# Sets of many products kept apart in a list schedule, and a GLU's tokens split anew for each group of f

## The chip, the cores and the metric

One Trainium2 chip, one core. The metric is the device time of one execution in microseconds, as a median over runs; one more execution was taken with the hardware profiler. Its engines are named as in the profile: PE (TensorE's matmuls), PEld (its weight loads), DVE (VectorE), ACT (ScalarE), POOL (GpSimd, here memsets and issuing DMAs) and SP (SyncE, here only issuing DMAs).

## The reference

A gate mixes a state-space convolution (S4D) with a bilinear GLU; L = 2048 tokens, D = 512 channels, N = 128 states, F = 1792:

```python
g = sigmoid((u * gate_w).sum(-1, keepdims=True))
P = exp((A * dt[:, None])[:, :, None] * pos)          # A, C complex, (D, N)
K = 2 * einsum("dn,dnl->dl", C, P).real               # the kernel of the convolution
a = irfft(rfft(u.T, 2 * L) * rfft(K, 2 * L))[:, :L].T + u * D_skip
b = ((x @ w_gate) * (x @ w_up)) @ w_down
return g * a + (1 - g) * b
```

All is float32.

## The kernel before

**The GLU.** x comes transposed (xT) in four blocks ci of 512 tokens, each as KT = 4 tiles of 128 x 512. Its products run in a faster float format (F32R) at three products each: every operand is split into a high part (ACT casts the loaded tile `raw` to `xhi`) and a low part (DVE subtracts: `xlo` = `raw` - `xhi`), and hi x lo, lo x hi and hi x hi are summed. The 14 tiles of f are taken in five groups of three or two (`GROUPS`); each group goes over all four ci, to and fro, so that of the four ci of a group after the first three need their tokens again. For each f, 24 products give `pg` and `pu` (gate and up), ACT and DVE make h = pg * pu and split it into `hh` and `hl`, and products with the split down weights (`dhi`, `dlo`) add up in `y`. Each group's y is scaled by 1 - g (`acc`) and stored to or added to the output in memory by a DMA; the last block's y is added in SBUF to what was loaded into `kt` (`ends`).

Where do the tokens come from? `tokens_first` (group 0) loads xT into `raw`, splits it, and POOL stores both halves in device memory (`x_d`). `tokens_again` (later groups) has SP load the two halves from `x_d`. `raw` has two buffers, shared with the loads of weights; `xhi` and `xlo` have five each.

**The convolution.** u goes through a first Fourier step (`u_part`, eight sets `k<-in,w_t`). For 16 blocks of 32 channels DVE and ACT build tables `x` and `v`, whose products make the convolution's kernel (`k_block`, `kgen`: `k<-v,x`). Every fourth block, `k_first` transforms it (`k<-kt,w1k_t`), and `transforms(q)` does the rest for a quarter q of the channels: four second steps (`m_second`: `k<-in,w2s`, in the last quarter `k<-v,w2s` with `k<-x,w2s`), the product of spectra on DVE, two inverse steps (`m_inverse`: `k<-y,w3s`), each followed by stores to `y_d`, loads from `y_d`, and two last steps (`m_last`: `k<-in,w_t`, in the last quarter `k<-v,w_t`). Then the gate is applied and POOL adds the result to the output.

A **set** is what one such task issues on TensorE. `kgen`, `m_second` and `m_inverse` issue 64 small float32 matmuls on parts of the array; the profile shows each as two pairs of a weight load and a matmul, so a set has 128 pairs. `k_first` issues sets of 16 and 48 pairs; `u_part` and `m_last` only 8.

**What sets the order.** Nothing is issued directly. `add` records a Task with an engine, an assumed time, tiles read and written, a rank and, for DMAs, kilobytes. `Work.run` is a list scheduler: it keeps a time for each engine and one for the bus, and of all tasks whose inputs are there and whose buffers come free it takes the one that can start first, then the lowest rank; GLU products have rank 2, sets 1, 0 or -1. The tasks are issued in that order, and each engine keeps it (`InOrder`). So the table of assumed times decides the order on every engine, and nothing else about the run.

Of the kernel before, what the change touches and what calls it, by code (L numbers as in the profile page):

```python
# [10 lines left out]
F32 = mybir.dt.float32  # L11
F32R = mybir.dt.float32r
# [6 lines left out]
P = 128  # L19
# [119 lines left out]
class Task:  # L139
    def __init__(self, n, engine, us, fn, rank, after, dma):  # L140
        self.n, self.engine, self.us, self.fn, self.rank, self.after, self.dma = n, engine, us, fn, rank, after, dma
        self.deps, self.tiles, self.start, self.end, self.rows = set(), [], None, None, ()


class Work:
# [10 lines left out]
    PE_LAG = 0.17  # L156

    OVERLAP = {"act": 0.09, "dve": 0.08}
    DMA_RATE = 0.3

    def __init__(self):
# [5 lines left out]
    def memory(self):  # L167
        return Tile(self, None, None, None, None, None, False)

    def add(self, engine, us, fn, r=(), w=(), rank=1, after=0.0, dma=0, hold=(), rows=()):  # L170


        task = Task(len(self.tasks), engine, us, fn, rank, after, dma)
        task.rows = rows
        self.tasks.append(task)
        clash = lambda p, q: p is None or q is None or p == q
        split = lambda x: x if isinstance(x, tuple) else (x, None)
        for tile, part in map(split, r):
            task.deps.update(t for p, t in tile.writers if clash(p, part))
        for tile, part in map(split, w):  # L180
            task.deps.update(t for p, t in tile.writers + tile.readers if clash(p, part))
        for tile, part in map(split, r):
            tile.readers.append((part, task))
        for tile, part in map(split, w):
            tile.writers.append((part, task))
        for tile, _ in map(split, [*r, *w, *hold]):
            if tile.pool and tile not in task.tiles:
                task.tiles.append(tile)
                tile.users.append(task)
        task.deps.discard(task)  # L190
        return task
# [34 lines left out]
    def run(self):  # L226
        left = {}
        for t in self.tasks:
            left.setdefault(t.engine, []).append(t)
        free = {e: 0.0 for e in left}  # L230
        bus, order, known, rows = 0.0, [], {}, {}
        while any(left.values()):
            best, wanted, found = None, {}, []
            for e, tasks in left.items():
                for t in tasks:
                    at = known.get(t)
                    if at is None:
                        at = self.inputs(t)
                        if at is None:
                            continue  # L240
                        known[t] = at
                    found.append((t, at))
                    for tile in t.tiles:
                        if tile.loose and tile.made is None:
                            wanted.setdefault(tile.key, []).append((t.rank, at))
            for t, ins in found:
                at = self.slots(t, ins)
                if at is None:
                    continue
                start = max([at, free[t.engine]] + [rows[r] for r in t.rows if r in rows])  # L250
                if any(
                    rank < t.rank and when <= start
                    for tile in t.tiles if tile.made is None and tile.loose for rank, when in wanted[tile.key]
                ):
                    continue
                key = (start, t.rank, t.n)
                if best is None or key < best[0]:
                    best = (key, t)
            assert best, "no work can start"
            (start, _, _), t = best  # L260
            left[t.engine].remove(t)
            t.start, t.end = start, start + t.us
            free[t.engine] = t.end - self.OVERLAP.get(t.engine, 0.0)
            if t.dma:
                bus = max(bus, t.end + 1.3) + t.dma / self.DMA_RATE / 1000
                t.end = bus + 0.5
            rows.update((r, t.end) for r in t.rows)
            for tile in t.tiles:
                if tile.made is None:
                    tile.made = start  # L270
                    tile.had.append(tile)
            order.append(t)
        for t in order:
            t.fn()
        return order
# [3 lines left out]
def gated_mix_kernel(  # L279
# [29 lines left out]
    su_d = dram.tile([KT, P, 32, P], F32, name="su_d")  # L309
    sk_d = dram.tile([KT, P, 32, P], F32, name="sk_d")  # L310
    y_d = dram.tile([KT, P, 32, P], F32, name="y_d")
    x_d = dram.tile([4, KT, 2, P, D], F32, name="x_d")
    m_su, m_sk, m_y, m_out = (work.memory() for _ in range(4))
    m_x = {}

    pools = {n: open_pool(n, b, PSUM) for n, b in (("ps_y", 2), ("ps_g", 1), ("ps_k", 4))}
    const = open_pool("const")
# [69 lines left out]
    def load_two(key, tile_of, src, one=True):  # L387

        t = tile_of([P, 2, D])
        for k in range(2):  # L390
            raws[key(k)] = (t, k)
        if one:
            add("sp", 0.42, lambda: sp.dma_start(t.t, src), w=[t], dma=512, rank=-1)
        return t
# [3 lines left out]
    def first_loads():  # L398
        in_y = lambda shape: new("mid", "y", shape, bufs=2)
        in_ev = lambda shape: new("mid", "ev", shape, bufs=3)  # L400
        xsrc = lambda kt: xT[P * kt : P * kt + P, :D]
        w0 = load_two(lambda k: ("w", 0, k), in_ev, None, False)
        x01 = load_two(lambda k: ("x", 0, k), in_y, None, False)
        for t, k, src in ((x01, 0, xsrc(0)), (w0, 0, wts[0][:, :D]), (w0, 1, wts[0][:, D : 2 * D]), (x01, 1, xsrc(1))):
            add("sp", 0.42, lambda t=t, k=k, src=src: sp.dma_start(t.t[:, k], src), w=[(t, k)], dma=256, rank=-1)
        x23 = xT[2 * P : 4 * P, :D].rearrange("(k p) t -> p k t", k=2)
        load_two(lambda k: ("x", 0, 2 + k), in_y, x23)
        for f in (1, 2):
            load_two(lambda k, f=f: ("w", f, k), in_ev, wts[f][:, : 2 * D].rearrange("p (k d) -> p k d", k=2))


        zero = new("glu", "acc", [P, D], bufs=3)
        scratch = bank()
        add("dve", 0.2, lambda: dve.memset(zero.t, 0.0), w=[zero], rank=-1)

        def warm():
            for _ in range(3):
                pe.matmul(scratch.t, zero.t[:, :P], zero.t, start=True, stop=True)

        add("pe", 4.0, warm, r=[zero], w=[scratch], rank=-1)  # L420

    def weights(fs):
        for f in fs:
            ws[f] = [new("glu", n, [P, 2 * D], F32R, len(GROUPS[0])) for n in ("whi", "wlo")]
            for c in range(2):
                load(("w", f, c), wts[f][:, c * D : (c + 1) * D])
                split(ws[f][0], ws[f][1], c, ("w", f, c))
            if f == 0:
                for kt in range(1, KT):
                    tokens_first(0, kt)  # L430

    def down_weights(fs):
        for f in fs:
# [1 line left out]
            load(("w", f, 2), wts[f][:, 2 * D :])  # L435
            split(wd[f][0], wd[f][1], None, ("w", f, 2))

    def tokens_first(ci, kt):

        x = xs[kt] = [new("glu", n, [P, D], F32R, 5) for n in ("xhi", "xlo")]  # L440
        load(("x", ci, kt), xT[kt * P : (kt + 1) * P, ci * D : (ci + 1) * D])
        split(x[0], x[1], None, ("x", ci, kt))
        for k in range(2):
            m = m_x[ci, kt, k] = work.memory()
            add("pool", 0.95, lambda k=k: pool_q.dma_start(x_d[ci, kt, k], x[k].t.bitcast(F32)), r=[x[k]], w=[m], dma=256)

    def tokens_again(ci, kt):
        x = xs[kt] = [new("glu", n, [P, D], F32R, 5) for n in ("xhi", "xlo")]
        for k in range(2):
            add(  # L450
                "sp", 0.42, lambda k=k: sp.dma_start(x[k].t.bitcast(F32), x_d[ci, kt, k]),
                r=[m_x[ci, kt, k]], w=[x[k]], dma=256, rank=0,
            )

    THREE = ((1, 0), (0, 1), (0, 0))

# [101 lines left out]

    def glu():
        order = [(gi, ci) for gi in range(len(GROUPS)) for ci in (range(4) if gi % 2 == 0 else range(3, -1, -1))]  # L560
        tokens_first(0, 0)
        weights(GROUPS[0])
        down_weights(GROUPS[0])
        old = 0
        for n, (gi, ci) in enumerate(order):
            fs = GROUPS[gi]
            if ci != old:
                for kt in range(KT):
                    (tokens_again if gi else tokens_first)(ci, kt)
            old = ci  # L570
            hs = {f: hidden(f) for f in fs}
            ends = n % 4 == 3 and gi + 1 < len(GROUPS)
# [346 lines left out]
    def k_block(b, x, v):  # L919
# [12 lines left out]
        if b % 4 == 0:  # L932
            kts["now"] = new("tab", "kt", [P, 64, 32])
        kt, g0 = kts["now"], b % 4 * 8
        add("pe", 2.15, kgen, r=[x, v], w=[pk], rank=0, hold=[kt])
        add(
            "act", 1.09,
            lambda: act.copy(
# [7 lines left out]
    def k_first(q, kt):  # L946

        tt(0.19, lambda: kt.t[:, 48, :], lambda: kt.t[:, 48, :], lambda: skip[:, q], ALU.add, [m_skip], [kt])
        for h in range(2):
# [14 lines left out]
                            )  # L964
                    to += n

            add("pe", 2.08, fn, r=[kt, m_w1k], w=banks, rank=-1, hold=sts)
            for half in range(2):

                st = sts[half]  # L970
# [56 lines left out]
    def m_second(q, ins, w):  # L1027
# [15 lines left out]
                                    start=True, stop=True, tile_position=(64 * e, 32 * j),  # L1043
                                )

        add("pe", 2.13, fn, r=[*ins, w], w=banks[0] + banks[1], rank=1, hold=tos)
        for which in range(2):
            for e in range(2):
                to, bk = tos[which], banks[which][e]
# [37 lines left out]
    def m_inverse(q, T0, ys, ws):  # L1087
# [14 lines left out]
                                    ys[t].t[lanes, k, e, cs], start=k == 0, stop=k == 1, tile_position=(32 * j, 64 * e),  # L1102
                                )

        add("pe", 2.13, fn, r=[*ys, *ws], w=banks, rank=1, hold=sts)
        for j in range(4):
            st, m = sts[j // 2], j % 2
            evict(
# [189 lines left out]
```

## Time and profile before

| | us |
|---|---|
| median of 3 runs (lowest to highest) | 633.33 (632.41 to 633.38) |
| the profiled execution's own time | 631.22 |
| its span, first to last instruction | 629.4 |
| PE's last product ends | 625.4 |
| DMA traffic | 142.63 MB, 227 GB/s |

Every instruction has line L100, that of the helper which issues it, so the profile is read by tile names: `out<-in`. "Issue" is time in which an engine waited for nothing that the profile shows. Matmuls overlap, so that a product's own duration (0.39 us) is longer than the distance from one to the next. In the chain in order of time, merged pieces give that distance: length divided by count.

### The profile page before, as it was taken

To read this page: it belongs to the slowest core of one execution; us is meant where nothing else is said; L and a number is where in the kernel's file an instruction comes from. 1 tells how busy PE (TensorE), PEld (TensorE's weight loads), DVE (VectorE), ACT (ScalarE), POOL (GpSimd) and SP (SyncE) were. 2 spreads that over 40 slices of the span, in tenths; PEclk is the share of its full clock that TensorE was granted. 3 is DMA by queue.
4 is the path that set the end of the run, shared out by engine and by line. 5 is a ranking of instruction groups with operands and counts; after the bars stand their busy time and mean duration, and the time that the engine had idled before them with its cause. 6 is when DMAs were issued, how large, how long until landed. Compare 5 with 4: busy or idle time off the path is not lost.

```text
span 629.4 us, 17934 instructions
## 1 busy us (share of the span) xinstructions
PE 608.8 (97%) x7526; PEld 469.1 (75%) x7526; DVE 486.1 (77%) x760; ACT 397.0 (63%) x903; POOL 106.1 (17%) x157
## 2 busy tenths in 40 slices
PE   7899999999999999999999999999999998999997
PEld 5667768688687787877777887778787676786885
DVE  6858999999999898999999999899853255632113
ACT  5379778968787764887977687796544542222220
POOL 3143332211021110202110101201010030102210
PEclk9999999999999999999999999999999999999999
DMA  8899868557879697969998398899889598958841
GB/s 310 266 338 334 298 191 317 180 164 238 231 184 284 179 240 224 223 200 257 196 321 219 93 247 264 210 222 275 242 239 326 171 245 215 280 152 193 161 68 67
DMA packets 111892, 142.63 MB, mean 227 GB/s; under 512 B 7876, under 2 KB 66756, under 8 KB 111556
## 3 DMA queue, kind: packets, MB, share of 16 engines
q1 hardware_dynamic: 90100, 105.05, 52.9%
q0 software_dynamic: 21568, 36.45, 28.1%
q8 instruction: 59, 0.97, 0.6%
q14 instruction: 21, 0.17, 0.1%
q10 hardware_dynamic: 144, 0.00, 0.0%
HBM read 81.96 MB, written 59.51 MB: 225 GB/s over the span
## 4 chain that ended last, share of the span: by engine, by line
PE 89%; DMA 5%; issue 2%; DVE 2%; ACT 1%; SPq 0%; ACTq 0%; DVEq 0%
PE pu L100 23%; PE pg L100 23%; PE y L100 23%; PE k L100 20%; DMA raw<-in_xT 2%; DMA raw<-in_wts 2%; DMA xlo<-x_d 1%; DVE x L100 1%; DMA small<-in_rows 1%; DVE kt L100 0%; ACT ts L100 0%; ACT acc L100 0%; ACT xhi L100 0%; ACT dhi L100 0%; SPq L100 0%
## 5 line engine op out<-in xcount | busy, mean ns | idle before, releaser
L100 POOL DMA_DIRECT2D out<-acc x60 | 51.4, 901 | 357.9 <-ACT acc L100 333.1
L100 PE MATMUL pg<-xhi,wlo 128*128 128x512 f32 x224 | 89.7, 401 | 2.9 <-DVE wlo L100 1.8
L100 PE MATMUL y<-dhi,hl 128*128 128x512 f32 x224 | 89.7, 401 | 2.7 <-DVE hl L100 2.4
L100 PE MATMUL pu<-xhi,wlo 128*128 128x512 f32 x224 | 90.1, 402 | 0.4 <-issue 0.4
L100 PE MATMUL pg<-xlo,whi 128*128 128x512 f32 x224 | 87.9, 392 | 1.9 <-issue 1.2
L100 PE MATMUL pu<-xlo,whi 128*128 128x512 f32 x224 | 87.4, 390 | 0.0
L100 PE MATMUL y<-dhi,hh 128*128 128x512 f32 x224 | 87.4, 390 | 0.0
L100 PE MATMUL pg<-xhi,whi 128*128 128x512 f32 x224 | 87.3, 390 | 0.0
L100 PE MATMUL y<-dlo,hh 128*128 128x512 f32 x224 | 87.3, 390 | 0.0
L100 PE MATMUL pu<-xhi,whi 128*128 128x512 f32 x224 | 87.3, 390 | 0.0
L100 DVE TENSOR_TENSOR h<-pu,h 128x512 f32<-128x512 f32 x56 | 38.5, 688 | 59.4 <-PE pu L100 58.3
L100 ACT ACTIVATE acc<-y,ngate 128x512 f32<-128x512 f32 x76 | 52.1, 690 | 34.6 <-PE y L100 31.7
L100 ACT CAST hh<-h 128x512 fp32r<-128x512 f32 x56 | 34.7, 620 | 59.6 <-DVE h L100 59.6
L100 ACT COPY ts<-k 128x512 f32<-128x512 f32 (+1 forms) x116 | 48.8, 497 | 19.9 <-PE k L100 19.9
L100 ACT COPY h<-pg 128x512 f32<-128x512 f32 x56 | 32.9, 588 | 41.8 <-PE pg L100 37.5
L100 PEld LDWEIGHTS pg<-xhi,wlo 128*128 128x128 f32 x224 | 42.0, 188 | 19.4 <-issue 5.0
L100 PEld LDWEIGHTS y<-dhi,hl 128*128 128x128 f32 x224 | 42.0, 187 | 17.9 <-DVE hl L100 4.1
L100 PEld LDWEIGHTS pu<-xhi,wlo 128*128 128x128 f32 x224 | 42.0, 187 | 17.3 <-issue 8.3
L100 PEld LDWEIGHTS pg<-xlo,whi 128*128 128x128 f32 x224 | 42.1, 188 | 11.6 <-issue 1.6
L100 PEld LDWEIGHTS pu<-xhi,whi 128*128 128x128 f32 x224 | 42.1, 188 | 9.1
L100 PEld LDWEIGHTS y<-dhi,hh 128*128 128x128 f32 x224 | 42.0, 188 | 9.1
L100 PEld LDWEIGHTS pg<-xhi,whi 128*128 128x128 f32 x224 | 42.1, 188 | 9.0
(105 smaller groups left out, 1127.6 us busy)
## 6 DMA issues: line engine op xcount, KB each, us to landing
out<-acc POOLq DMA_DIRECT2D x60, 256.0 KB, 6.0
xhi<-x_d SPq DMA_DIRECT2D x48, 256.0 KB, 5.1
xlo<-x_d SPq DMA_DIRECT2D x48, 256.0 KB, 5.2
raw<-in_wts SPq DMA_DIRECT2D x36, 256.0 KB, 4.6
su_d<-ts POOLq DMA_DIRECT2D x32, 256.0 KB, 5.1
sk_d<-ts SPq DMA_DIRECT2D x16, 512.0 KB, 4.6
y_d<-ts SPq DMA_DIRECT2D x16, 512.0 KB, 5.7
in<-sk_d SPq DMA_DIRECT2D x12, 512.0 KB, 6.4
```

The source lines that it names most:

```text
L100: got = getattr(self.engine, name)(*args, **kw)
```

## The change

A task can be marked `many`. `kgen`, `k_first`, `m_second` and `m_inverse` are. The scheduler keeps a time `apart`: a marked task doesn't start before the end of the last marked one plus `APART` = 4.0 us of its own clock. And `tokens_first`, `tokens_again`, `x_d` and its stores go; one function `tokens` loads xT and splits it in every group (`raws` is a table of loads already asked for, so the group is now part of its key).

```diff
+    APART = 4.0
...
-        task.rows = rows
+        task.rows, task.many = rows, many
...
-                start = max([at, free[t.engine]] + [rows[r] for r in t.rows if r in rows])
+                start = max([at, free[t.engine], apart * t.many] + [rows[r] for r in t.rows if r in rows])
...
             left[t.engine].remove(t)
+            if t.many:
+                apart = start + t.us + self.APART
...
-    def tokens_first(ci, kt):
+    def tokens(gi, ci, kt):
         x = xs[kt] = [new("glu", n, [P, D], F32R, 5) for n in ("xhi", "xlo")]
-        load(("x", ci, kt), xT[kt * P : (kt + 1) * P, ci * D : (ci + 1) * D])
-        split(x[0], x[1], None, ("x", ci, kt))
-        for k in range(2):
-            m = m_x[ci, kt, k] = work.memory()
-            add("pool", 0.95, lambda k=k: pool_q.dma_start(x_d[ci, kt, k], x[k].t.bitcast(F32)), r=[x[k]], w=[m], dma=256)
-
-    def tokens_again(ci, kt):
-        x = xs[kt] = [new("glu", n, [P, D], F32R, 5) for n in ("xhi", "xlo")]
-        for k in range(2):
-            add(
-                "sp", 0.42, lambda k=k: sp.dma_start(x[k].t.bitcast(F32), x_d[ci, kt, k]),
-                r=[m_x[ci, kt, k]], w=[x[k]], dma=256, rank=0,
-            )
+        load(("x", gi, ci, kt), xT[kt * P : (kt + 1) * P, ci * D : (ci + 1) * D])
+        split(x[0], x[1], None, ("x", gi, ci, kt))
...
-                    (tokens_again if gi else tokens_first)(ci, kt)
+                    tokens(gi, ci, kt)
...
-        add("pe", 2.15, kgen, r=[x, v], w=[pk], rank=0, hold=[kt])
+        add("pe", 2.15, kgen, r=[x, v], w=[pk], rank=0, hold=[kt], many=True)
...
-            add("pe", 2.08, fn, r=[kt, m_w1k], w=banks, rank=-1, hold=sts)
+            add("pe", 2.08, fn, r=[kt, m_w1k], w=banks, rank=-1, hold=sts, many=True)
...
-        add("pe", 2.13, fn, r=[*ins, w], w=banks[0] + banks[1], rank=1, hold=tos)
+        add("pe", 2.13, fn, r=[*ins, w], w=banks[0] + banks[1], rank=1, hold=tos, many=True)
...
-        add("pe", 2.13, fn, r=[*ys, *ws], w=banks, rank=1, hold=sts)
+        add("pe", 2.13, fn, r=[*ys, *ws], w=banks, rank=1, hold=sts, many=True)
```

Since the scheduler's clock decides the order of everything, the order moves on all engines from the start on. Three places, with the names of the program and their buffer numbers.

On PE before, in the first quarter's transforms (at 236.77 us of the profile), a `kgen` set, six GLU products, and the first products of an `m_second` set:

```order
L100 MATMUL k_3084<-v_639,x_2306 32x64 x64
L100 MATMUL pg_3064<-xhi_2310,wlo_2696 128x512
L100 MATMUL pg_3064<-xlo_2316,whi_2688 128x512
L100 MATMUL pg_3064<-xhi_2310,whi_2688 128x512
L100 MATMUL pg_3064<-xhi_2322,wlo_2696 128x512
L100 MATMUL pg_3064<-xlo_2325,whi_2688 128x512
L100 MATMUL pg_3064<-xhi_2322,whi_2688 128x512
L100 MATMUL k_3176<-in_2806,w2s_2802 32x128
```

On PE after, at a like place in the first quarter: a `kgen` set, and the first 11 of the products behind it:

```order
L100 MATMUL k_2698<-v_626,x_2003 32x64 x64
L100 MATMUL y_2776<-dhi_1607,hl_2535 128x512
L100 MATMUL y_2776<-dlo_1621,hh_2517 128x512
L100 MATMUL y_2776<-dhi_1607,hh_2517 128x512
L100 MATMUL y_2776<-dhi_1613,hl_2640 128x512
L100 MATMUL y_2776<-dlo_1625,hh_2636 128x512
L100 MATMUL y_2776<-dhi_1613,hh_2636 128x512
L100 MATMUL pg_2642<-xhi_2272,wlo_2433 128x512
L100 MATMUL pg_2642<-xlo_2296,whi_2430 128x512
L100 MATMUL pg_2642<-xhi_2272,whi_2430 128x512
L100 MATMUL pg_2642<-xhi_2325,wlo_2433 128x512
L100 MATMUL pg_2642<-xlo_2339,whi_2430 128x512
```

Behind these, seven more GLU products follow, 18 in all, and then the next set (`k<-y,w3s`). Nowhere in the new order do fewer than 18 products stand between two marked sets that follow each other with nothing but GLU products between.

On PE before, the last quarter's `m_last` (the k products) with the GLU products around it:

```order
L100 MATMUL pu_7944<-xlo_7874,whi_6869 128x512
L100 MATMUL pu_7944<-xhi_7871,whi_6869 128x512
L100 MATMUL k_7959<-v_7708,w4_t_92 64x512 x2
L100 MATMUL k_7962<-v_7708,w4_t_92 64x512 x2
L100 MATMUL k_7972<-v_7708,w4_t_92 64x512 x2
L100 MATMUL k_7975<-v_7708,w4_t_92 64x512 x2
L100 MATMUL pg_7982<-xhi_7450,wlo_7000 128x512
L100 MATMUL pg_7982<-xlo_7452,whi_6998 128x512
L100 MATMUL pg_7982<-xhi_7450,whi_6998 128x512
```

On PE after, the end of the program, from the same k products on:

```order
L100 MATMUL k_8291<-v_8116,w4_t_91 64x512 x2
L100 MATMUL k_8294<-v_8116,w4_t_91 64x512 x2
L100 MATMUL k_8298<-v_8116,w4_t_91 64x512 x2
L100 MATMUL k_8301<-v_8116,w4_t_91 64x512 x2
L100 MATMUL y_8308<-dhi_6684,hl_8121 128x512
L100 MATMUL y_8308<-dlo_6698,hh_8111 128x512
L100 MATMUL y_8308<-dhi_6684,hh_8111 128x512
L100 MATMUL y_8308<-dhi_6691,hl_8218 128x512
L100 MATMUL y_8308<-dlo_6706,hh_8216 128x512
L100 MATMUL y_8308<-dhi_6691,hh_8216 128x512
L100 MATMUL y_8308<-dhi_6897,hl_8267 128x512
L100 MATMUL y_8308<-dlo_6899,hh_8261 128x512
```

Before, 192 GLU products stood behind these k products, now nine (the last of them, hi x hi, is cut off here); 48 stand between them and the last inverse set.

On SP before, the end of the queue from the last stores to `y_d` on (`out<-kt` and three pairs of loads from `x_d` follow):

```order
L100 DMA y_d_59<-ts_7782 128x8x128
L100 DMA y_d_59<-ts_7789 128x8x128
L100 DMA xhi_7853<-x_d_60 128x512
L100 DMA xlo_7858<-x_d_60 128x512
L100 DMA xhi_7860<-x_d_60 128x512
L100 DMA xlo_7865<-x_d_60 128x512
L100 DMA xhi_7871<-x_d_60 128x512
L100 DMA xlo_7874<-x_d_60 128x512
L100 DMA xhi_7881<-x_d_60 128x512
L100 DMA xlo_7887<-x_d_60 128x512
L100 DMA v_7708<-y_d_59 32x4096 x2
```

On SP after, the end of the queue:

```order
L100 DMA raw_7753<-in_xT 128x512
L100 DMA w2s_7765<-in_w2 128x512
L100 DMA kt_7800<-out_0 128x2048
L100 DMA w3s_7993<-in_w3 128x512
L100 DMA w3s_8001<-in_w3 128x512
L100 DMA y_d_59<-ts_7990 128x8x128
L100 DMA y_d_59<-ts_7998 128x8x128
L100 DMA v_8116<-y_d_59 32x4096 x2
L100 DMA y_d_59<-ts_8223 128x8x128
L100 DMA y_d_59<-ts_8229 128x8x128
L100 DMA v_8116<-y_d_59 32x4096 x2
L100 DMA out_0<-kt_7800 128x512 x4
```

The loads from `x_d` are gone, and loads of xT stand further ahead; the two trips through `y_d` (store, then load into `v`) now stand directly ahead of the last stores to the output.

On DVE and ACT, 48 subtracts `xlo<-raw,xhi` and 48 casts `xhi<-raw` more stand among the work of groups 1 to 4; on POOL, 32 DMAs `x_d<-xhi` and `x_d<-xlo` are gone.

More of the change, by code (lines that the diff above doesn't have):

```diff
@@ L141, in __init__ @@
         self.n, self.engine, self.us, self.fn, self.rank, self.after, self.dma = n, engine, us, fn, rank, after, dma
-        self.deps, self.tiles, self.start, self.end, self.rows = set(), [], None, None, ()
+        self.deps, self.tiles, self.start, self.end, self.rows, self.many = set(), [], None, None, (), False
 class Work:
@@ L168, in memory, with add @@
         return Tile(self, None, None, None, None, None, False)
-    def add(self, engine, us, fn, r=(), w=(), rank=1, after=0.0, dma=0, hold=(), rows=()):
+    def add(self, engine, us, fn, r=(), w=(), rank=1, after=0.0, dma=0, hold=(), rows=(), many=False):
         task = Task(len(self.tasks), engine, us, fn, rank, after, dma)
-        task.rows = rows
+        task.rows, task.many = rows, many
         self.tasks.append(task)
@@ L230, in run @@
         free = {e: 0.0 for e in left}
-        bus, order, known, rows = 0.0, [], {}, {}
+        bus, order, known, rows, apart = 0.0, [], {}, {}, 0.0
         while any(left.values()):
@@ L311, in gated_mix_kernel @@
     y_d = dram.tile([KT, P, 32, P], F32, name="y_d")
-    x_d = dram.tile([4, KT, 2, P, D], F32, name="x_d")
     m_su, m_sk, m_y, m_out = (work.memory() for _ in range(4))
-    m_x = {}
     pools = {n: open_pool(n, b, PSUM) for n, b in (("ps_y", 2), ("ps_g", 1), ("ps_k", 4))}
@@ L402, in first_loads @@
         w0 = load_two(lambda k: ("w", 0, k), in_ev, None, False)
-        x01 = load_two(lambda k: ("x", 0, k), in_y, None, False)
+        x01 = load_two(lambda k: ("x", 0, 0, k), in_y, None, False)
         for t, k, src in ((x01, 0, xsrc(0)), (w0, 0, wts[0][:, :D]), (w0, 1, wts[0][:, D : 2 * D]), (x01, 1, xsrc(1))):
@@ L406, in first_loads @@
         x23 = xT[2 * P : 4 * P, :D].rearrange("(k p) t -> p k t", k=2)
-        load_two(lambda k: ("x", 0, 2 + k), in_y, x23)
+        load_two(lambda k: ("x", 0, 0, 2 + k), in_y, x23)
         for f in (1, 2):
@@ L429, in weights @@
                 for kt in range(1, KT):
-                    tokens_first(0, kt)
+                    tokens(0, 0, kt)
     def down_weights(fs):
@@ L560, in glu @@
         order = [(gi, ci) for gi in range(len(GROUPS)) for ci in (range(4) if gi % 2 == 0 else range(3, -1, -1))]
-        tokens_first(0, 0)
+        tokens(0, 0, 0)
         weights(GROUPS[0])
```

## Prediction

> **What bounds the kernel now.** I read the page first, for who is busy and how the clock stood; then the table of TensorE's waits; then the chain in order of time, for how long clean work takes; and last TensorE's timeline at the places where it stood still.
>
> ```profile
> span 629.4 us, 17934 instructions
> PE 608.8 (97%) x7526; PEld 469.1 (75%) x7526; DVE 486.1 (77%) x760; ACT 397.0 (63%) x903; POOL 106.1 (17%) x157
> DVE  6858999999999898999999999899853255632113
> PEclk9999999999999999999999999999999999999999
> DMA packets 111892, 142.63 MB, mean 227 GB/s; under 512 B 7876, under 2 KB 66756, under 8 KB 111556
> q8 instruction: 59, 0.97, 0.6%
> PE k L100 <- issue: 7.0, 8, 1.9
> PE y L100 <- DVE hl L100: 2.4, 1, 2.4
> PE pg L100 <- DVE wlo L100: 1.8, 1, 1.8
> PE pg L100 <- issue: 1.2, 1, 1.2
> PE pg L100 <- ACT h L100: 1.2, 1, 1.2
> ```
>
> TensorE is at work 97% of the span at full clock, so only its standstills, its waits and the tail can move the time. Its data waits are few (2.4, 1.8, 1.2). The largest item is "issue": eight waits of 7.0 us in front of k products and one of 1.2 in the GLU, with no semaphore behind them. The next rows show what they are: first the chain in order of time (clean work), then TensorE's timeline.
>
> ```profile
> 209.70 2.72 PE pu L100 x12
> 217.18 1.99 PE k L100 x126
> 550.16 2.02 PE k L100 x125
> 577.57 3.58 PE k L100 x16
> 620.98 4.40 PE y L100 x18
> 625.41 0.76 DVE kt L100
> 204.19 0.92 PE L100 MATMUL k<-in,w2s 64*32 64x128 f32 x46
> 206.62 1.49 PE L100 MATMUL k<-in,w2s 64*32 64x128 f32 x82 [1.51 <-issue]
> 208.04 0.50 PE L100 MATMUL pg<-xhi,wlo 128*128 128x512 f32 x1
> 240.74 1.27 PE L100 MATMUL k<-in,w2s 64*32 64x128 f32 x66
> 243.19 1.13 PE L100 MATMUL k<-in,w2s 64*32 64x128 f32 x62 [1.18 <-issue]
> 533.23 1.14 PE L100 MATMUL k<-v,w2s 64*32 64x128 f32 x63
> 536.32 0.50 PE L100 MATMUL y<-dhi,hl 128*128 128x512 f32 x1
> 156.54 2.07 PE L100 MATMUL k<-v,x 128*32 128x64 f32 x128
> 160.72 0.39 PE L100 MATMUL pg<-xhi,wlo 128*128 128x512 f32 x1
> 162.32 0.50 PE L100 MATMUL pg<-xlo,whi 128*128 128x512 f32 x1 [1.21 <-issue]
> ```
>
> Clean, a GLU product takes 2.72 / 12 = 0.227 us and a set of 128 pairs (weight load and matmul) 2.0 us. The set at 204.19 ends at 208.04: 3.85 us, so 1.85 were lost in its middle, behind pair 46. I read this as instructions arriving late. Queue q8 brought 0.97 MB in 59 packets, 16.4 KB each; the span has 2 x 7526 = 15,052 weight loads and matmuls, so one is about 64 bytes and a packet about 256 of them, 128 pairs: as much as one set. Between the stop behind pair 46 at 204.19 and the one behind pair 66 at 240.74 stand 762 pairs, all but six times 128 (waiting instructions are the rest). So the stops sit on the borders of fetched **blocks**. A block costs about 29 us of GLU time to run through, but 2 us within a set; if two borders are passed faster than a fetch takes, TensorE stands. The row at 162.32 shows that one set alone suffices: the set began at 156.54, only ten products followed, and 1.2 us were lost.
>
> **The change, part by part.** TensorE's products are the same before and after; only their order moves.
>
> *1. Sets apart.* Before, 15 sets follow another with 3 to 15 products between; after, none with fewer than 18 (4.1 us). Eight of the 15 ran long: those at 204.19, 236.77, 240.74, 310.05, 338.47, 444.35, 450.48 and 533.23 (first and last: 3.85 and 3.09 us, rows above) take 23.7 us together instead of 16.0: 7.7 us. Another 3.8 us are lost in four sets further apart, 1.4 in the GLU at 162.32: 12.8 in all. To see what remains, I counted blocks off both orders, a border every 256 instructions from the one behind pair 46, and gave each its clean time. Before, 14 blocks take under 4.2 us (8.8 us lost, 0.63 each) and 15 take 4.2 to 7 (4.0 lost, 0.26 each). After, 7 and 20: the closest pairs have gone, but a set whose ends fall on two borders is still a 2 us block. At these rates 7 x 0.63 + 20 x 0.26 = 9.6 us remain. I take a quarter off, since the fetch shares its DMA engines with 15% fewer bytes (part 2): 7.2. Result **-5.6 us**; ends -12.8 (no stop left) and 0 (as many as before).
>
> [...]
>
> *2. Tokens split anew.*
>
> ```profile
> xhi<-x_d SPq DMA_DIRECT2D x48, 256.0 KB, 5.1
> xlo<-x_d SPq DMA_DIRECT2D x48, 256.0 KB, 5.2
> raw<-in_xT SPq DMA_DIRECT2D x12, 256.0 KB, 4.8
> L100 ACT CAST xhi<-raw x12: 602/622/647, 29.3 to 96.5; 128x512 fp32r<-128x512 f32 x12
> L100 DVE TENSOR_TENSOR xlo<-raw,xhi x12: 681/687/692, 29.9 to 97.1; 128x512 fp32r<-128x512 f32 x12
> 300.00:450.00 150.00, 148.34 (x2581) 115.74 (x2580) 143.25 (x212) 115.66 (x280) 18.94 (x20) 1.00 0.91 231
> 450.00:530.00 80.00, 77.27 (x1039) 58.99 (x1044) 39.67 (x61) 33.98 (x72) 10.10 (x10) 1.00 0.87 232
> ```
>
> The 32 stores of halves (POOL) go, and 96 loads from x_d become 48 from xT on SP: 80 transfers of 256 KB fewer, 21 MB of the 142.6. Added are 48 casts (48 x 0.622 = 29.9 us of ACT) and 48 subtracts (48 x 0.687 = 33.0 us of DVE). At the start, up to 100 us, the stores' 8.4 MB and POOL's issues go while TensorE waits for weights and h (2.4 + 1.8 + 1.2 = 5.4 us of waits): **-1.2**, ends -3 and +1. In the middle DVE is full: 143.25 of 150 us in the last long window, so 7 us free, and the 33 us push table work later; behind 450 us it has 80 - 39.7 = 40 us free. The cover is TensorE's GLU work, which the new order puts ahead of the late tables. I take **+0.5** for small waits, ends 0 and +5: without that cover, each us of DVE would be a us of TensorE.
>
> *3. The end.* The last set, the two inverse sets ahead of it and the store and load through y_d move back: before, 192 GLU products stand behind the last k products (44 us from 581.15), after, 9 (2.0 us).
>
> ```profile
> out<-ts POOLq DMA_DIRECT2D x7, 512.0 KB, 7.7
> y_d<-ts SPq DMA_DIRECT2D x16, 512.0 KB, 5.7
> v<-y_d SPq DMA_DIRECT2D x4, 512.0 KB, 7.7
> out<-ts POOLq DMA_DIRECT2D x1, 256.0 KB, 4.5
> out<-kt SPq DMA_DIRECT2D x4, 256.0 KB, 2.0
> ```
>
> Between the last inverse and the last k products stand 48 products after, 48 x 0.227 + 0.2 = 11.1 us. Within it, four evictions (1.5 us by the two engines), the store (5.7) and the load (7.7) must pass: 15 us by the medians, under a load that will be thinner at the end. So TensorE waits, and with it everything behind: between 0 (both transfers in 9.5) and 4 us; **+1.8**. And the tail: before, the span ends 629.4 - 625.4 = 4.0 us after the last product, by one short store (2.0). After, two accumulating stores on POOL start about 2.5 and 0.5 us ahead of TensorE's end; with 7.7 and 4.5 us to land, and 0.9 that now lie behind the last landing, they end 6.1 and 4.9 us after it. I take 5.3: **+1.3**, ends 0 and +2.5.
>
> Sum against the profiled execution: 631.2 - 5.6 - 1.2 + 0.5 + 1.8 + 1.3 = 628.0 us. The median of the runs is 633.3, 2.1 above that execution, so I put the median at **630.0 us**.
>
> **Rivals.**
> - *The fetch stops stay* (also: the change doesn't do what it says). What they cost would hang on where borders fall, not on distance. For it: 162.32, and four long sets over 4 us from any other; against it: eight of the twelve long sets follow closely. Part 1 gives 0: 633.6 in the profile, 635.7 as a median. [...]
> - *The chain at the end takes over*, slower than before. Place: the store and load through y_d ahead of the last k products. Price: each us beyond the 11.1 of cover, once more in the tail. With the trip of the profile before (inverse over at 552.2, last k products at 577.57: 25 us, held there by other loads on SP) as the upper end and 18 us as a likely one, the wait is 7 instead of 1.8: 635.2. It decides from a trip of 17.5 us: the sum without the wait is 628.2, and 6.4 of wait make it 634.6.
> - *Nearly no stop is left*: part 1 gives -11, with the thinner DMA load: 624.6.
> - *DVE sets the pace* between 300 and 450 us: +4 of its 33 us come through: 633.5, no change.
>
> **How the numbers follow.** Forecast (625 to 632): 0.52. Few stops left: 0.14. Equal, by DVE or a small part 1: 0.15. Stops stay: 0.09. End chain: 0.10. Two measurements of this kernel differ by about 0.2%, 1.3 us, and that is the bound for "the same": 632.0 to 634.6. Faster 0.66, same 0.15, slower 0.19. The range takes in the second rival's time and its price, and most of the case with few stops: 622.0 to 636.5. The forecast's own range is 625 to 632.
>
> **What would show it.** Right: "issue" ahead of k products falls from 7.0 to 2 to 5 us; where a stop remains, it sits behind a whole number of blocks, mostly in or just behind a set that is alone. DVE near 519 us and ACT near 427 busy, 121 to 122 MB moved, no x_d. TensorE's last product some 5 us ahead of the span's end, and a wait of 0 to 4 us in front of the last k products, ended by v<-y_d. Wrong: new waits of TensorE for DVE or a load in the middle of more than 3 us together; a wait in front of the last k products over 5 us; "issue" at 7 us or more.

## The result and the profile after

| | before | after |
|---|---|---|
| median of the runs, us (lowest to highest) | 633.38 (632.41 to 637.11) | 627.43 (627.06 to 630.09) |
| ratio, with 95% interval | | 0.991 (0.9882 to 0.9939) |
| profiled execution: own time, span | 631.22, 629.4 | 627.43, 625.7 |
| TensorE's last product ends | 625.4 | 617.0 |
| tail behind it | 4.0 | 8.7 |
| TensorE's waits named "issue", together | 8.6 | 2.7 |
| DMA traffic, MB | 142.63 | 121.67 |

The change made the kernel 0.9% faster; 630.0 was predicted, with a range of 622.0 to 636.5. TensorE is done 8.4 us earlier, and more than half of that is lost again behind its last product. From the page of the changed kernel:

```profile
span 625.7 us, 17973 instructions
...
PE 607.1 (97%) x7526; PEld 468.4 (75%) x7526; DVE 513.7 (82%) x808; ACT 421.7 (67%) x951; POOL 88.8 (14%) x125
...
DMA packets 102422, 121.67 MB, mean 194 GB/s; under 512 B 6596, under 2 KB 65476, under 8 KB 102084
```

DVE and ACT carry the 48 new subtracts and casts (486.1 and 397.0 before). Its table of TensorE's waits (total us, how often, the longest):

```profile
PE y L100 <- issue: 1.8, 1, 1.8
...
PE pg L100 <- DVE wlo L100: 1.0, 1, 1.0
PE k L100 <- PE y L100: 1.0, 1, 1.0
PE k L100 <- ACT kt L100: 0.9, 1, 0.9
PE pg L100 <- issue: 0.9, 1, 0.9
PE pg L100 <- ACT h L100: 0.8, 2, 0.5
PE k L100 <- DMA in<-in_u: 0.5, 1, 0.5
```

"Issue" in front of k products is gone (7.0 before); two such waits remain, in the GLU, 2.7 us. The start's waits fell from 5.4 us (2.4, 1.8, 1.2) to 2.3 (wlo 1.0, h 0.8, in_u 0.5). TensorE's timeline shows the larger remaining stop:

```profile
214.33 2.07 PE L100 MATMUL k<-v,x 128*32 128x64 f32 x128
216.33 0.50 PE L100 MATMUL y<-dhi,hl 128*128 128x512 f32 x1
216.67 0.39 PE L100 MATMUL y<-dlo,hh 128*128 128x512 f32 x1
216.90 0.40 PE L100 MATMUL y<-dhi,hh 128*128 128x512 f32 x1
219.06 0.50 PE L100 MATMUL y<-dhi,hl 128*128 128x512 f32 x1 [1.77 <-issue]
```

A set that stands alone, three products, then 1.77 us of nothing. Between this stop and the other one (383.48) stand 2416 products, each with its weight load, and 32 waiting instructions: 2 x 2416 + 32 = 4864 = 19 x 256. Both sit on borders of blocks. Now the end, first the chain in order of time:

```profile
603.53 3.41 PE y L100 x15
...
607.77 2.38 PE y L100 x9
610.15 0.95 issue
611.10 3.65 PE k L100 x16
614.75 2.28 PE y L100 x9
```

The wait in front of the last k products is 0.95 us. The table above puts it down to PE y, which had ended when the wait began; it is the second load of `v`, which was issued at 606.11 and landed at 610.90. The next rows show how long the transfers of the end took: the table of DMA issues, with the median time to landing.

```profile
out<-ts POOLq DMA_DIRECT2D x7, 512.0 KB, 8.3
...
v<-y_d SPq DMA_DIRECT2D x4, 512.0 KB, 4.9
...
out<-kt SPq DMA_DIRECT2D x4, 256.0 KB, 5.8
...
out<-ts POOLq DMA_DIRECT2D x1, 256.0 KB, 8.9
```

And the timelines of SP's and POOL's DMA issues:

```profile
602.64 3.79 SPq L100 DMA_DIRECT2D v<-y_d  x2
...
614.06 2.88 POOL L100 DMA_DIRECT2D out<-ts  x2 [30.96 <-DVE ts L100]
...
615.83 4.40 SPq L100 DMA_DIRECT2D out<-kt  x4
```

The k products begin at 611.10, 0.2 us behind that landing. Behind the last product (617.0) the span runs 8.7 us on. Two accumulating stores, issued on POOL from 614.06 for 2.88 us, and the four short stores `out<-kt` are under way at once: the median `out<-kt` takes 5.8 us instead of 2.0, and the last one lands at 624.75, as the last transfer of all.

### The profile page after: what moved, and what is told of

Read it like the earlier page. It is cut to its first block, busy times and chain, and to the rows that moved or that the text cites. A ratio compares the mean times of both kernels' runs of the same rounds, so it can differ in the third digit from the quotient of the medians.

```text
span 625.7 us, 17973 instructions
## 1 busy us (share of the span) xinstructions
PE 607.1 (97%) x7526; PEld 468.4 (75%) x7526; DVE 513.7 (82%) x808; ACT 421.7 (67%) x951; POOL 88.8 (14%) x125
## 2 busy tenths in 40 slices
DMA packets 102422, 121.67 MB, mean 194 GB/s; under 512 B 6596, under 2 KB 65476, under 8 KB 102084
## 4 chain that ended last, share of the span: by engine, by line
PE 79%; DVE 6%; DMA 5%; issue 5%; ACT 3%; SPq 0%; ACTq 0%; DVEq 0%; POOLq 0%
PE y L100 21%; PE pu L100 20%; PE pg L100 20%; PE k L100 18%; DMA out<-acc 2%; DMA raw<-in_wts 2%; DVE v L100 1%; DMA in<-in_u 1%; DVE x L100 1%; DMA ev<-in_wts 1%; DVE h L100 1%; DVE hl L100 1%; DVE wlo L100 1%; ACT acc L100 1%; DVE xlo L100 0%
## 5 line engine op out<-in xcount | busy, mean ns | idle before, releaser
L100 POOL DMA_DIRECT2D out<-acc x60 | 53.2, 943 | 351.3 <-ACT acc L100 337.8
L100 PE MATMUL y<-dhi,hl 128*128 128x512 f32 x224 | 91.5, 408 | 2.8 <-issue 1.8
```

The costliest lines, as they stand in the source:

```text
L100: got = getattr(self.engine, name)(*args, **kw)
```

## The experiments

Twelve kernels, all timed against the kernel before on the same chip. "Issue" is the sum of TensorE's issue waits in the profiled execution, which isn't always a typical one: in `apart5` it took 625.10 us and in `end_free` 630.31, the fastest of its runs. The last column counts blocks off the order, a border every 256 instructions, each block at its clean time: under 3 us (all or nearly all of a set lies in one block), 3 to 4.2 us, 4.2 to 7 us; the last two kernels were not counted.

| kernel | median us | ratio to before (95%) | issue us | tail us | blocks |
|---|---|---|---|---|---|
| before | 633.4 | | 8.6 | 4.0 | 2, 12, 15 |
| after | 627.4 | 0.991 (0.988 to 0.994) | 2.7 | 8.7 | 4, 3, 20 |
| split_only | 638.9 | 1.009 (1.006 to 1.012) | 10.9 | 4.1 | 2, 10, 14 |
| apart_only | 628.6 | 0.991 (0.989 to 0.994) | 7.1 | 4.0 | 5, 2, 23 |
| apart5 | 627.8 | 0.990 (0.986 to 0.993) | 1.7 | 4.1 | 3, 4, 7 |
| end_free | 635.3 | 1.001 (0.998 to 1.005) | 9.6 | 4.1 | 5, 4, 18 |
| store_later | 622.6 | 0.983 (0.979 to 0.986) | 2.9 | 4.3 | 3, 3, 19 |
| store_later_2 | 638.5 | 1.011 (1.004 to 1.018) | 12.0 | 4.3 | 4, 8, 15 |
| before_shift | 643.3 | 1.015 (1.011 to 1.019) | 15.2 | 4.1 | 4, 10, 11 |
| after_shift | 639.4 | 1.007 (1.004 to 1.010) | 10.0 | 8.6 | 6, 4, 16 |
| store_later_shift | 644.5 | 1.012 (1.008 to 1.016) | 17.7 | 4.3 | 6, 2, 17 |
| store_later_block | 625.9 | 0.989 (0.984 to 0.993) | 3.1 | 4.3 | 4, 3, 19 |
| before_pad32 | 648.1 | 1.023 (1.018 to 1.028) | 13.2 | 4.1 | |
| run_of_sets | 652.0 (one run) | | 17.3 | 4.1 | |

### Each part alone

`split_only` is the changed kernel with the sets not kept apart:

```diff
-    APART = 4.0
+    APART = 0.0
```

> The changed kernel with APART = 0: tokens split anew, sets not kept apart (14 sets follow another within 15 GLU products, as 15 did before); in its order 132 GLU products stand behind the last k products. Theory (distance between sets removes the stops): stops at borders of fetched blocks stay at 8 to 13 us, the tail is about 4.0 us as before, the split itself moves the time by -1 to +2 us: 627 to 633 us as a median against 633.4 before, and slower than or about equal to the changed kernel. Rival (the thinner DMA traffic, 122 MB instead of 143, removes the stops, the distance does nothing): stops fall to about 5 us as in the changed kernel and the short tail stays: about 623 us.

It is slower than before, and above the range of either theory. The thinner traffic does not remove the stops: 10.9 us of issue waits (6.5, 3.0 and 1.4 in its table of waits):

```profile
PE k L100 <- issue: 6.5, 5, 2.0
PE pg L100 <- issue: 3.0, 1, 3.0
PE k L100 <- ACT kt L100: 1.8, 1, 1.8
PE pg L100 <- DVE xlo L100: 1.7, 1, 1.7
...
PE pu L100 <- issue: 1.4, 1, 1.4
```

Added to that are waits for split tokens and tables (xlo 1.7, kt 1.8), which the changed kernel has at 0.3 and 0.9. `apart_only` is the kernel before with the four marks and APART = 4.0, x_d kept:

> The kernel before with the four marks and APART = 4.0, but with x_d as before (143 MB moved); 168 GLU products behind the last k products. Theory (distance): stops fall from 12.8 to about 5 us, tail 4.0 us as before, nothing else changes: about 625 to 626 us, faster than the changed kernel, whose tail is 8.7 us. Rival (traffic): 10 to 13 us of stops remain, 631 to 633 us. Both share in it: 7 to 9 us remain, 628 to 630 us.

628.6 us: sets apart alone give what the whole change gives (0.991), and not all of the stops go. With the split the time is 5.5 us longer where the sets are not apart (638.9 - 633.4); where they are, the 1.2 us between 628.6 and 627.4 are within the intervals, with a tail 4.7 us longer. Not all of either number need be the split's own: it changes the order, and with it the places of the borders, which the shifts below price at 10 us and more.

### What a stop is

In `run_of_sets` one set of the kernel before runs six times in a row:

```diff
-            for d in range(TB):
+            for d in [*range(TB)] * (6 if b == 8 else 1):
```

> The kernel before, in which the ninth k<-v,x set (about 330 us into the span) issues its 64 products six times over, one run directly behind the other, so that 768 pairs stand in a row; the repeated ones write the same values again, the order of all else is the same. It measures what a block of 256 instructions costs when nothing covers its fetch. Theory (a block is fetched only when the one ahead of it is entered, and comes 2 to 5 us later): the run takes 3.0 to 4.5 us a block instead of 2.0, with a stop of 1 to 2.5 us at every border of the five or six inside it; six sets take 18 to 27 us, and the kernel 16 to 25 us longer. Rival (fetches run far enough ahead, and the stops seen come from something that closely following different sets share): 12.0 to 12.5 us for the run, the kernel 10 us longer. After stops of 1.9 to 3.9 us the earlier runs showed in some places a granted clock of 0.50 for 3 to 4 us; if stops bring it, it shows here too.

TensorE's timeline there:

```profile
295.80 1.92 PE L100 MATMUL k<-v,x 128*32 128x64 f32 x117
300.33 3.16 PE L100 MATMUL k<-v,x 128*32 128x64 f32 x128 [2.61 <-issue]
303.78 2.33 PE L100 MATMUL k<-v,x 128*32 128x64 f32 x128 [0.29 <-issue]
307.23 2.04 PE L100 MATMUL k<-v,x 128*32 128x64 f32 x128 [1.13 <-issue]
310.96 2.04 PE L100 MATMUL k<-v,x 128*32 128x64 f32 x128 [1.68 <-issue]
314.69 0.90 PE L100 MATMUL k<-v,x 128*32 128x64 f32 x43 [1.68 <-issue]
```

One kind of product, no semaphore, and a stop every 128 pairs: 3.45 to 3.73 us a block instead of 2.0. The run takes 19.7 us (to 315.5) where 12 were work, and the kernel is 17.8 us longer (652.0 against 634.2 in that session). The windows show why the second block (3.16 us of busy time) seems to have hardly a stop, and how loaded the DMA engines were (us, PE busy with its count, granted clock, DMA share, GB/s):

```profile
300.00:304.00 4.00, 3.38 (x137) 0.63 0.02 7
304.00:308.00 4.00, 2.87 (x182) 0.95 0.01 4
308.00:312.00 4.00, 2.32 (x162) 1.00 0.01 4
```

Behind the first stop of 2.61 us the clock fell (0.63 from 300 to 304 us). And the DMA engines stood nearly idle (share 0.01 to 0.02): 3.45 to 3.73 us a block is what a fetch takes from border to border with hardly any other traffic. The traces say the same of every other stop. In the fourteen profiles TensorE has 101 issue waits. Counted in the order of its weight loads, matmuls and waiting instructions, every one ends at instruction 193 or 194 (the first counts as 0) or a whole number of 256 behind it, and 1.2 to 1.6 us after a 16 KB packet of the instruction queue (q8) has landed. `before_pad32` and `before_shift` move the borders by half a block against the products, the first by small products behind the warm-up, the second by repeating half of one set:

```diff
+            for _ in range(32):
+                pe.matmul(scratch.t[:, :1], zero.t[:, :P], zero.t[:, :1], start=True, stop=True)
```

```diff
-            for d in range(TB):
+            for d in [*range(TB), *range(16 if b == 0 else 0)]:
```

> The kernel before with 32 one-column float32 products (64 pairs, 128 instructions, half a fetched block) added behind the warm-up products on TensorE, ahead of the first GLU product; the order of everything else is the same. Theory (stops sit on borders of blocks of 256 instructions): every border moves 64 pairs back. The stop behind pair 46 of the first second-step set (204.19 in the profile before) is gone, and one stands behind pair 110 of that set instead; the one behind pair 66 of the set at 240.74 moves to pair 2 of it. The sum of the stops stays 9 to 16 us, the time within 3 us of before. Rival (the stops belong to the products themselves: to a switch of array position, to a bank or to data): they stay behind pairs 46 and 66.

> The kernel before, in which the first k<-v,x set (131.83 in the profile before) issues its first 32 products twice: 64 pairs or half a block more, all small products at full clock, and about 1 us more work; the order of all else is the same. Every later border of a block moves 64 pairs back against the products, as in the run with the products added at the start, without that run's loss of clock there. Theory: no stop at the old places (behind pair 46 of the set at 204.19, pair 66 at 240.74), stops at the places where the run before_pad32 had its, 10 to 18 us of them; the time is 630 to 640 us, by luck of the places. Rival (stops belong to the products): the old places, and 634 us.

`before_pad32` missed its time: 648.1 us, 14.7 above before, most of it lost at the start (see the last section). Its stops had moved, though: the first of them stands behind pair 119 of the `k<-v,x` set ahead (215.08), and none behind pair 46. (In `before_shift` the repeated set is in fact the one at 83.56 of the profile before, not at 131.83.) The timeline of `before_shift` at the two places named:

```profile
203.53 1.97 PE L100 MATMUL k<-v,x 128*32 128x64 f32 x119
...
209.43 0.65 PE L100 MATMUL k<-v,x 128*32 128x64 f32 x9 [3.93 <-issue]
...
214.15 2.11 PE L100 MATMUL k<-in,w2s 64*32 64x128 f32 x101
...
248.97 0.40 PE L100 MATMUL k<-in,w2s 64*32 64x128 f32 x3
250.49 2.02 PE L100 MATMUL k<-in,w2s 64*32 64x128 f32 x125 [1.12 <-issue]
```

The stop that stood behind pair 46 of a `k<-in,w2s` set now stands behind pair 119 of the `k<-v,x` set ahead of it, 55 pairs and nine GLU products earlier: 64. The next one went from behind pair 66 to behind pair 3 of its set. The stop expected at pair 110 did not come: the granted clock was 0.50 from 208.3 to 215.1 us (GLU products 0.43 us apart), so that the block in between took 6.7 us, more than the 3.45 to 3.73 us of a fetch in `run_of_sets`. Products, data and order are the same: the stops belong to the blocks. But the time is 643.3, 10 us more than before and above the expected range. A shift that was meant only to move stops changed their sum from 8.6 to 15.2 us. So the same shift was put on the changed kernel, and on the best one (below):

> The changed kernel with the same shift as before_shift: the first k<-v,x set (79.86 in its profile) issues its first 32 products twice, so that every later border moves 64 pairs back against the products; about 1 us more work. Theory (with the sets apart few borders fall badly, wherever they lie): stops of 4 to 9 us, 628 to 633 us, so that of the gain over before some is left and against before_shift (643) it is 10 us or more. Rival (the changed kernel merely drew good places for its borders): stops of 10 to 18 us, 633 to 643 us.

> The kernel of store_later (groups 3 and 4 load their halves, APART = 4.0) with the same shift at the first k<-v,x set (80.40 in its profile). Theory (distance): stops of 4 to 9 us instead of about 5, 623 to 628 us. Rival (good places by luck): stops of 10 us or more, 629 to 638 us.

Here the rival held: 639.4 us, and 644.5, which is above even the rival's range. The control repeats the whole set instead of half of it, which brings the borders back to the same products:

> The control for the shifts: the kernel of store_later, in which the first k<-v,x set issues all 64 of its products twice, so that every later border moves by a whole block of 256 instructions and falls on the same products as in store_later again. More products are repeated than in store_later_shift (644.5 us), not fewer. Theory (the shifts cost time by where the borders come to lie): 2.0 us more work and one stop of 1 to 3 us behind the repeated set, the later stops as in store_later (about 5 us): 625 to 630 us. Rival (the repeated products themselves, by the clock or by moving everything 1 us later against the transfers, bring the loss): 636 us or more.

625.9 us, 2.0 of the 3.3 above `store_later` being the repeated work. So it is the place of the borders that costs, not the repetition. What such a place costs shows in `store_later_shift`, first in TensorE's timeline:

```profile
332.32 2.06 PE L100 MATMUL k<-in,w2s 64*32 64x128 f32 x128
334.30 0.50 PE L100 MATMUL pg<-xhi,wlo 128*128 128x512 f32 x1
...
335.10 0.40 PE L100 MATMUL pu<-xhi,wlo 128*128 128x512 f32 x1
338.63 0.40 PE L100 MATMUL pu<-xlo,whi 128*128 128x512 f32 x1 [3.13 <-issue]
```

and in windows, columns as above:

```profile
332.00:335.00 3.00, 3.00 (x133) 1.00 0.91 111
335.00:338.60 3.60, 0.50 (x3) 1.00 1.01 222
...
340.00:341.00 1.00, 1.00 (x3) 0.50 1.13 349
```

The block is 128 pairs: all but the first four of the set and the four products behind it. It was entered at 332.4 and left at 338.6: 6.2 us with the DMA engines full (share 0.91 to 1.01), against 3.45 to 3.73 with idle ones. From 1.2 us after the stop the granted clock is 0.50 for 3.4 us, and GLU products stand 0.43 us apart instead of 0.23: part of the stop is paid a second time.

### The end, and how far apart

> The changed kernel with APART = 5.0 instead of 4.0. Its order has 99 GLU products behind the last k products instead of 9, and 7 blocks of 256 instructions that take under 4.2 us and 7 of 4.2 to 7 us instead of 7 and 20. Theory (tail and stops each cost as read): tail 4 to 5 us instead of 8.7, no wait in front of the last k products, stops 3 to 5 us instead of 5, about 1.5 us lost where TensorE waits for data near 250 us: about 622 to 624 us. Rival for the tail (it is long because DVE and the stores are late in the changed kernel wherever the k products stand): tail stays 8 to 9 us, about 627 us.

The tail is 4.1 us, with `out<-kt` at 2.0 again, and issue waits are 1.7. But its runs spread from 622.55 to 629.36 us (one took 631.95), their mean granted clock from 1.000 down to 0.995, and the median of 627.8 lies above the expected range; the profiled execution, of 625.1, isn't a typical one. The rival for the tail is out, the expected time was missed. In `end_free` the sets of the last quarter lose their marks (`many=q < KT - 1`, and `many=b < 12` for `kgen`):

> The changed kernel with the marks left off in the last quarter of channels: its order has 54 GLU products behind the last k products instead of 9, and 75 between the last inverse set and them instead of 48. Theory (the tail and the wait in front of the last k products come from the apart rule pushing the end of the chain back): tail 4.0 to 4.5 us instead of 8.6, no wait in front of the last k products instead of 1.0; the sets of the last quarter stand closer, which gives back 1 to 4 us of stops; 622 to 626 us. Rival (the tail is the late stores' own, wherever the k products stand): tail 7 to 9 us, 627 us or more.

Tail 4.1 and no wait in front of the last k products, so that part is settled; but the closer sets brought 9.6 us of issue waits, and nothing is left of the gain. `store_later` takes the work off DVE instead: group 2 stores its split halves, groups 3 and 4 load them.

```diff
+        if gi in (3, 4) and (ci, kt, 0) in m_x:
+            for k in range(2):
+                add("sp", 0.42, lambda k=k: sp.dma_start(x[k].t.bitcast(F32), x_d[ci, kt, k]), r=[m_x[ci, kt, k]], w=[x[k]], dma=256, rank=0)
+            return
         load(("x", gi, ci, kt), xT[kt * P : (kt + 1) * P, ci * D : (ci + 1) * D])
         split(x[0], x[1], None, ("x", gi, ci, kt))
+        if gi == 2:
+            for k in range(2):
+                m = m_x[ci, kt, k] = work.memory()
+                add("pool", 0.95, lambda k=k: pool_q.dma_start(x_d[ci, kt, k], x[k].t.bitcast(F32)), r=[x[k]], w=[m], dma=256)
```

> The changed kernel, APART = 4.0, in which group 2's split halves are stored to x_d by POOL and groups 3 and 4 load them instead of splitting anew: 24 casts and 24 subtracts fewer (DVE about 497 us busy instead of 514), about 130 MB moved instead of 122. Its order has 114 GLU products behind the last k products instead of 9. Theory (the end is late in the changed kernel because the extra work on DVE pushes the tables of the last quarter back, and the apart rule adds to that): tail 4.0 us, no wait in front of the last k products, stops 4 to 8 us: 621 to 625 us. Rival (traffic matters more for the stops than distance): stops 8 to 10 us, 625 to 628 us.

From its page, and from its table of TensorE's waits:

```profile
PE 607.2 (98%) x7526; PEld 469.1 (76%) x7526; DVE 502.2 (81%) x788; ACT 410.3 (66%) x931; POOL 102.2 (16%) x149
```

```profile
PE y L100 <- issue: 1.6, 1, 1.6
...
PE k L100 <- issue: 1.3, 2, 1.1
```

622.6 us, 0.983 of before and the best of all here: DVE and ACT lose 11.5 and 11.4 us, the tail is 4.3, and the stops stay at 2.9 although 11.5 MB more are moved. The same kernel with APART = 2.0 and the same end:

> The kernel of store_later with APART = 2.0 instead of 4.0, nothing else: the planner sees the same end for TensorE within 0.3 us, the traffic is the same, and 99 products stand behind the last k products. 12 blocks of 256 instructions take under 4.2 us in its order and 15 take 4.2 to 7 us, instead of 6 and 19. Theory (the distance between sets is what removes the stops): stops of 9 to 16 us instead of 5, 627 to 636 us. Rival (the thinner traffic, or the end, made the gain): 621 to 625 us, as store_later.

638.5 us, above the range of either theory, with 12.0 us of issue waits, one of 4.8 us. In this pair only the distance rule differs, and with it the order and the places of the borders: 16 us for both together, which this pair can't tell apart.

## Why the prediction was right, and where it was not

**The reading of "issue"** as instructions that come late is shown: by `run_of_sets` (a stop every 128 pairs), by the shifts (the stops stay on the borders, whatever stands there) and by the packets that land 1.2 to 1.6 us ahead of each stop's end. Most borders bring no stop (49 of 59 in `before` have no issue wait); where a block is short, one can come: in `run_of_sets` a block takes 3.45 to 3.73 us for 2.0 us of work, with nearly idle DMA engines (share 0.01 to 0.02).

**1. Sets apart** (-5.6). The issue waits fell by 5.9 us (8.6 to 2.7). Counted as in the prediction, by the excess over clean time, the stops fell from 12.8 to about 5 us (1.9 at 219.06, 1.1 at 383.48, the rest under 1 us each), so by nearly 8. The mechanism was right, the size a little small (-5.6 forecast). What was wrong is the price of a short block: one rate was taken for all under 4.2 us, and for how many there would be, one place of the borders was read as if it were typical. Nor does any run support the quarter taken off for the thinner traffic (`split_only` has that traffic and 10.9 us of issue waits). Read off afterwards, in the kernels with APART of 4 or 5 the issue waits go with the blocks under 3 us, those that hold nearly a whole set: 3, 3, 4, 5, 6 and 6 of them in apart5, store_later, after, apart_only, after_shift and store_later_shift, with 1.7, 2.9, 2.7, 7.1, 10.0 and 17.7 us (end_free, with its last sets close, has 5 and 9.6, store_later_block 4 and 3.1).

Half a block of shift is worth 10 to 22 us of time (1 us of it the added products), more than the whole change. The first rival (cost by where borders fall, chance 0.09) was therefore half right. Counted in the two orders over all places that the borders could have, blocks of 3 to 4.2 us fall from 12.0 on average to 3.8, while those under 3 us stay at 3.0: distance removes the pairs of sets, and luck decides on the sets alone in a block. Nor does every short block stop: the one of 2.0 us at 472.55 of the changed kernel, with GLU products ahead of it, had no stop behind it, and the last packet had landed 1.9 us before it began.

At each of the two places measured the changed kernel is the faster one, by 627.4 against 633.4, and by 639.4 against 643.3 (1.007 and 1.015 of before, measured in different sessions); `store_later_shift`, with its sets apart too, has 1.012 and gains hardly anything there. Other places were not run.

**2. Tokens split anew** (-1.2 and +0.5). At the start 3.1 us were gained (5.4 to 2.3 of waits). In the middle the data waits seen are kt 0.9 and four of 0.2 to 0.4, 2.2 us together and about 1.7 more than before, against +0.5 forecast: the cover by GLU work held, within the stated 0 to 5. In `split_only`, with the old distances, the same 33 us of DVE work come with 3.5 us of waits for kt and xlo. That the two parts depend on each other, which the step left out, is a reading of these waits and was not tested by itself. DVE at 513.7 and ACT at 421.7 are within 6 us of the forecast.

**3. The end** (+1.8 and +1.3). The wait in front of the last k products was 0.95, and `v<-y_d` took 4.9 us where 7.7 were put in, so the rival of the end chain did not come. The DMA share there was 0.68 (600 to 612 us), against 0.84 around before's last load (556 to 578), which had eight loads from `x_d` issued just ahead of it; that the thinner traffic shortened the load fits, and was not tested. The tail is the term that was mis-sized: +4.7 (4.0 to 8.7) instead of +1.3. The step gave the late accumulating stores 7.7 and 4.5 us, as if alone, and took `out<-kt` as in before, where it needs 2.0; under way together they took 7.1, 8.9 and 5.8, and an `out<-kt` landed last. `apart5`, `end_free` and `store_later`, with 99, 54 and 114 GLU products behind the last k products instead of 9, end 4.1 to 4.3 us behind TensorE, with `out<-kt` at 2.0: the stores were late because the k products were.

**Sum.** -7 to -8 (stops), -3.1 (start), +1.7 (middle), +1.0 (wait), +4.7 (tail) make -2.7 to -3.7; the span moved by -3.7. The medians moved by -6.0, since the profiled execution of before was 2.2 us below its median and that of the changed kernel was at it. That 630.0 came near 627.4 is luck in part, by errors that offset each other: a gain of 6.8 was forecast for stops and start and 10 to 11 came, against losses of 3.6 forecast and 7.4 that came.

**Still open:** what the thinner traffic is worth. A single block took longer in a busy stretch (6.2 against 3.7 us), but not every one did: in `before_shift`, blocks of 2.0 us of work that ended in stops took 3.2 and 3.7 us (86.88 and 543.29) at DMA shares of 0.88 and 1.01. And `apart_only` (142.64 MB, 7.1 us) and `after` (121.67 MB, 2.7 us) differ also in where their borders fall, and `store_later` has 2.9 us at 133.20 MB.

## What to carry to other kernels

Where TensorE runs through instructions much faster in some tasks than in others, read the place of one stop off a profile, mark every 256th instruction from there in the final order (all 101 issue waits of the fourteen profiles end on such a border), and give each block its clean time. A block that takes less than a fetch can bring a stop (here 2.0 us of work, where a fetch took 3.45 to 3.73 us with nearly idle DMA engines and 6.2 us in one place with full ones), so sets of many small instructions should be kept apart by more than that. A time measured at one alignment says little about such a change, since half a block of shift was worth 10 to 22 us here: shift the borders by half a block, with a whole block as control, before 1% is believed. And look at what a rule that pushes work back does to the end of the program: here its last stores came together with the others, and the tail grew by 4.7 us.

## What the runs showed of the hardware

**A stop can be paid again in clock.** After several stops of 1.9 us and more the granted clock fell to 0.50 for 3.4 us (`split_only`, 1.90 us of idle at 322.47, with a set of small products just ahead of it: from 323.1 to 326.5; `store_later_shift`, 3.13 us: from 339.8 to 343.2) or twice that (`before_shift`, 3.93 us: from 208.3 to 215.1). That costs about half of such a stretch, with GLU products 0.43 us apart instead of 0.23. After others of up to 3.18 us (`apart_only` at 516.53, granted clock 1.00 from 500 to 550 us) it did not.

**Products of one column did not hold the clock.** In `before_pad32`, the 32 one-column products, 64 pairs, kept TensorE busy without a pause from about 6.7 us until the first GLU product at 17.15, and the granted clock fell while they ran, in windows of 4 us and one of 5:

```profile
8.00:12.00 4.00, 4.00 (x34) 0.88 1.02 357
12.00:16.00 4.00, 4.00 (x20) 0.50 1.03 414
16.00:20.00 4.00, 4.00 (x14) 0.50 1.04 408
20.00:25.00 5.00, 5.00 (x20) 0.87 0.28 107
```

Before, the clock is 1.00 throughout these windows. It isn't every small product: in `run_of_sets` the pairs of `k<-v,x` (64 columns) ran from 308 to 316 us at a granted clock of 1.00, with stops between. TensorE's wait for h at 47.17 of before came at 57.27 here: 10 of this kernel's 14.7 us (648.1 against 633.4) were lost at the start. Its time therefore shows nothing about the sum of the stops; it shows where they sit.
